# Which PSUM bank a tile gets: the one freed last, or the one that has been free longest

## Chip, cores and metric

The kernel runs on one core of a Trainium2 chip. The metric is the time of one execution on the device in microseconds (us), taken as the median of several runs. The core's engines are named as in the profile: PE (TensorE's matmuls), PEld (TensorE's weight loads), DVE (VectorE), ACT (ScalarE), POOL (GpSimd) and SP (SyncE, which here issues the DMAs).

## What is computed

Three blocks follow each other: an attention with RMS norms on q and k, a gated MLP that mixes over tokens, and a token and channel mixer. Batch 4, 12 heads of 64, 448 tokens, model width 768.

```python
q_n, k_n = (rmsnorm(q, g_q), rmsnorm(k, g_k))
scores = scale * np.matmul(q_n, k_n.transpose(0, 1, 3, 2))
attn = np.exp(scores - np.max(scores, axis=-1, keepdims=True))
x = np.matmul(attn / (np.sum(attn, axis=-1, keepdims=True) + 1e-09), v)
...
h = np.maximum(x @ w_in, 0.0)
u, v = (h[..., :d_ff // 2], h[..., d_ff // 2:])
v_s = np.einsum('ts,bsd->btd', w_spatial, layernorm(v)) + b_spatial[None, :, None]
x = (u * v_s) @ w_out
...
u = x + (np.maximum(x.transpose(0, 2, 1) @ w_tok1, 0.0) @ w_tok2).transpose(0, 2, 1)
out = u + np.maximum(u @ w_ch1, 0.0) @ w_ch2
```

## The kernel before

The kernel is not issued as it is written. Each engine call (`nc.tensor.matmul` and so on) is recorded by `Plan.add` (line 159) as an operation with an estimated cost and its dependencies. At the end `Plan.issue` (line 383) lays all operations out in time with a list scheduler, `Plan.place` (line 267), which gives each operation a planned start, and then emits every operation in the order of those starts. All instructions are emitted at line 424, so the profile shows L424 everywhere, and tiles tell the groups apart. Each engine runs its own instructions in that fixed order; between engines only semaphores hold them.

A matmul or a transpose writes a PSUM tile. PSUM has eight banks, and each tile takes one (`Banks`, line 129; `ALL` is 8). `place` hands the banks out: when an operation is about to write the first of a tile, it picks a bank from `free_banks`, a list of pairs (planned time from which the bank is free, bank number); when the last user of a tile is placed, the bank goes back on the list with the time at which that user is planned to be done. The tile is then allocated under the name `bank0` to `bank7` with one buffer each, so that on the chip the first write of a tile waits until all readers of the tile that had this bank before are done. `OWN` reserves four banks for kind "sc", two for "tp" and two for "mm"; a tile of one kind may take a bank beyond its share only while the others keep theirs. The pick is made in lines 332 to 341:

```python
free_banks.sort()
at = free_banks[len(ks) - 1][0]
if at > t:
    heapq.heappush(due[e], (at, i))
    continue
for k in ks:
    n = max(x for x in free_banks if x[0] <= t)
    free_banks.remove(n)
    bank[k] = n[1]
```

The stages, with the PSUM tiles that the profile names:

- Attention (`Attention.slot`, 24 pairs of heads): `sc` are the scores, read by DVE (maximum, `nm`) and by ACT (exponential, `e`); `tp` are transposes, read mostly by ACT into `et`, `over` or `whole` (the transposed q and k); `av` are the values.
- The gated MLP (`moe`), merged into the attention: `vps`, `ups` (read by ACT into `tg`), `sps` (read by DVE), `xps` (read by ACT into `xo`).
- The token mixer (`Tokens`): `h1ps` (read by ACT and DVE into `h`), `u_ps` (added by DVE into `x`), and `tp`.
- The channel mixer: seven products of a Strassen scheme, in `up` (line 1279) with tiles `h2ps`, which DVE adds into the blocks `c`, and in `down` (line 1325) with tiles `o_ps`, which DVE adds into `o` or `u`. `up` has 7 products times 2 batches times 6 tiles, 84 tiles of 9 matmuls each; `down` has 49 tiles of 18 matmuls. Their operands `op` come from ACT (high part) and DVE (low part), and so do the weights `w`. `word` is DVE's conversion of weights, merged into this and the earlier stages. Tiles in `up` and `down` take banks of the kinds "sc", "tp", "sc", "mm" in turn.

Of the kernel before, what the change touches and what calls it, by code (L numbers as in the profile page):

```python
# [110 lines left out]
class Pool:  # L111
# [5 lines left out]
    def tile(self, shape, dtype, tag, name, bufs=2):  # L117
        ring = self.tags.setdefault(tag, [])
        place = f"{tag}_{len(ring) % bufs}"
        t = Planned(lambda: self.pool.tile(shape, dtype, tag=place, bufs=1, name=name))  # L120
        if len(ring) >= bufs:
            t.after = ring[-bufs].users
        elif self.fence is not None:
            t.after = [self.fence]
        ring.append(t)
        return Part(t, shape, dtype)
# [23 lines left out]
class Plan:  # L150
# [116 lines left out]
    def place(self, before, after, lag, weight, tiles=None):  # L267
# [11 lines left out]
        if tiles is not None:  # L279
            opens, closes, users = tiles  # L280
            users = dict(users)
            free_banks = [(0.0, n) for n in range(Banks.ALL)]
# [6 lines left out]
        while placed < len(ops):  # L289
            t, e = min(  # L290
                (free_at[e] if waiting[e] else max(free_at[e], due[e][0][0]), e)
                for e in engines if waiting[e] or due[e])
            free_at[e] = t
            while due[e] and due[e][0][0] <= t:
                i = heapq.heappop(due[e])[1]
                heapq.heappush(waiting[e], (weight[i], i))
            i = heapq.heappop(waiting[e])[1]
            if e == "tensor" and ops[i].parts != parts:

                near = [x for x in waiting[e] if ops[x[1]].parts == parts and x[0] <= weight[i] + NEAR]  # L300
                if not near and parts and not ops[i].parts:
                    near = [x for x in waiting[e] if ops[x[1]].parts and x[0] <= weight[i] + NEAR]
                if near:
                    x = min(near)
                    waiting[e].remove(x)
                    waiting[e].append((weight[i], i))
                    heapq.heapify(waiting[e])
                    i = x[1]
            other = SHARED.get(e)
            if ops[i].port and port <= t and other in due and free_at[other] <= t:  # L310

                free_at[other] = t
                while due[other] and due[other][0][0] <= t:
                    x = heapq.heappop(due[other])[1]
                    heapq.heappush(waiting[other], (weight[x], x))
                if waiting[other] and waiting[other][0][0] < weight[i] and ops[waiting[other][0][1]].port:
                    heapq.heappush(waiting[e], (weight[i], i))
                    e = other
                    i = heapq.heappop(waiting[e])[1]
            if ops[i].port:  # L320
                if port > t:
                    heapq.heappush(due[e], (port, i))
                    continue
                port = t + ops[i].cost
            if tiles is not None and i in opens:
                ks = opens[i]
                kind = ks[0].psum
                spare = len(free_banks) - sum(max(0, n - held[x]) for x, n in Banks.OWN.items() if x != kind)
                if spare < len(ks):
                    blocked.append(i)  # L330
# [4 lines that stand above are left out]
                    heapq.heappush(due[e], (at, i))  # L335
                    continue
                for k in ks:
                    n = max(x for x in free_banks if x[0] <= t)
                    free_banks.remove(n)
                    bank[k] = n[1]  # L340
                held[kind] += len(ks)
            placed += 1
            start[i] = t
            end = t + ops[i].cost
            if e == "tensor":
                end += SWITCH * (ops[i].parts != parts)
                parts = ops[i].parts
            free_at[e] = end
            for s, hop in zip(after[i], lag[i]):
                ready[s] = max(ready[s], end + hop)  # L350
                left[s] -= 1
                if not left[s]:
                    heapq.heappush(due[ops[s].engine], (ready[s], s))
            if tiles is not None:
                for k in closes.get(i, ()):
                    users[k] -= 1
                    if not users[k]:
                        at = end + ops[i].late + TO["tensor"]
                        free_banks.append((at, bank[k]))
                        held[k.psum] -= 1  # L360
                        for x in blocked:
                            heapq.heappush(due["tensor"], (at, x))
                        blocked = []
# [1128 lines left out]
```

## Time and profile before

| | us |
|---|---|
| median of 3 runs | 887.33 |
| the runs | 885.97 to 889.61 |
| the profiled execution, its own time | 887.2 |
| its span, first to last instruction | 885.0 |
| PE busy in the span | 865.1 (98%) |
| DVE, ACT, POOL busy | 681.0, 537.1, 412.4 |

The profile is of one execution. A matmul's end in it is modelled: matmuls overlap, so that one instruction seems to last longer than the step from its start to the next one's start. Idle time of PE is counted from such an end, and a wait is put down to the instruction whose semaphore ended it. Times in views are counted from the start of the span.

### The profile page before, as it was taken

What the parts mean: (1) busy time and instruction counts of PE and PEld (TensorE: products, weight loads), DVE (VectorE), ACT (ScalarE), POOL (GpSimd) and SP (SyncE); (2) the same over time, 40 slices, a digit from 0 to 9 for tenths busy, and PEclk for the clock granted to TensorE, in tenths of its full rate; (3) what the DMA queues carried; (4) which work ended last, traced back from release to release, by engine and by line L of the source; (5) the groups of instructions that cost most, each with busy time, mean ns of one, the idle gap of its engine ahead of it and who ended that gap; (6) DMA issues with size and microseconds to landing.
All of it is one profiled execution on the core that took longest, in us unless ns stands there. A gap on an engine that the chain in (4) does not pass through costs nothing.

```text
span 885.0 us, 15472 instructions
## 1 busy us (share of the span) xinstructions
PE 865.1 (98%) x5018; PEld 718.2 (81%) x5018; DVE 681.0 (77%) x1333; ACT 537.1 (61%) x1278; POOL 412.4 (47%) x541
## 2 busy tenths in 40 slices
PE   7999999999999999999999999999999999999998
PEld 5444567678777787776889999998989999999998
DVE  5799798987777767866366567889889886998973
ACT  5999988778867867866453356555325654343331
POOL 3555655786666646574234123224324108514560
PEclk8999999999999999999999999999999999999999
DMA  6555665566644575344687678776554745661441
GB/s 153 138 148 172 198 185 149 161 183 211 182 131 127 152 216 169 103 128 127 225 252 236 195 227 268 220 245 202 161 160 138 227 125 170 197 188 54 143 152 63
DMA packets 153263, 152.27 MB, mean 172 GB/s; under 512 B 77152, under 2 KB 136352, under 8 KB 153184
## 3 DMA queue, kind: packets, MB, share of 16 engines
q1 hardware_dynamic: 152224, 151.06, 57.2%
q8 instruction: 40, 0.66, 0.3%
q10 hardware_dynamic: 960, 0.23, 0.1%
q14 instruction: 39, 0.32, 0.1%
HBM read 112.44 MB, written 38.80 MB: 171 GB/s over the span
## 4 chain that ended last, share of the span: by engine, by line
PE 79%; DVE 8%; ACT 4%; issue 3%; DMA 3%; POOL 2%; SPq 1%; DVEq 0%; POOLq 0%; ACTq 0%
PE h2ps L424 15%; PE o_ps L424 15%; PE tp L424 9%; PE av L424 7%; PE sc L424 7%; PE vps L424 7%; PE xps L424 6%; PE ups L424 6%; PE sps L424 4%; PE h1ps L424 2%; PE u_ps L424 2%; DVE word L424 1%; DVE c L424 1%; DVE op L424 1%; DVE w L424 1%
## 5 line engine op out<-in xcount | busy, mean ns | idle before, releaser
L424 PE MATMUL h2ps<-op,w 128*128 128x448 f32 x756 | 155.5, 367 | 2.0 <-DVE c L424 2.0
L424 PE MATMUL o_ps<-w,op 128*128 128x384 f32 x882 | 153.6, 334 | 1.6 <-DVE u L424 1.6
L424 PEld LDWEIGHTS o_ps<-w,op 128*128 128x128 f32 x882 | 152.8, 188 | 2.3 <-ACT op L424 1.5
L424 PEld LDWEIGHTS h2ps<-op,w 128*128 128x128 f32 x756 | 141.3, 188 | 14.7 <-DVE c L424 3.7
L424 ACT ACTIVATE e<-sc,nm 112x448 f32<-112x448 f32 x192 | 122.5, 654 | 22.6 <-DVE nm L424 22.3
L424 DVE TENSOR_REDUCE nm<-sc 112x1 f32<-112x448 f32 x192 | 109.4, 614 | 19.6 <-PE sc L424 19.0
L424 POOL TENSOR_TENSOR src<-src 128x384 f32<-128x384 f32 x48 | 61.1, 1283 | 76.5 <-DMA src<-c_d 55.2
L424 ACT ACTIVATE op<-c 128x768 fp32r<-128x768 f32 x49 | 41.5, 847 | 85.5 <-PE o_ps L424 81.9
L424 PEld LDWEIGHTS tp<-ident,e 112*128 112x128 f32 x672 | 72.3, 140 | 24.3 <-ACT et L424 7.2
L424 POOL TENSOR_SCALAR e<-e,sums 112x448 f32<-112x448 f32 x112 | 73.8, 676 | 36.9 <-DVE sums L424 21.2
L424 PE MATMUL tp<-ident,e 112*128 112x112 f32 x672 | 87.1, 262 | 1.9 <-ACT over L424 1.5
L424 ACT ACTIVATE et<-tp 128x448 f32<-128x448 f32 x144 | 71.2, 527 | 18.2 <-PE tp L424 15.6
L424 DVE TENSOR_SCALAR word<-word 128x256 f32<-128x256 f32 (+5 forms) x132 | 57.9, 448 | 24.5 <-ACT word L424 23.4
L424 POOL TENSOR_TENSOR u<-u,o 128x384 f32<-128x384 f32 x28 | 40.3, 1457 | 69.2 <-ACT o L424 38.9
L424 DVE SCALAR_TENSOR_TENSOR word<-raw,word 128x256 uint32<-128x256 uint32 (+2 forms) x132 | 70.7, 541 | 1.3
L424 PE MATMUL ups<-xp,wu 128*128 128x448 f32 x288 | 67.8, 375 | 0.4 <-ACT et L424 0.4
L424 DVE TENSOR_TENSOR op<-c,op 128x768 fp32r<-128x768 f32 x49 | 58.1, 1185 | 10.3 <-ACT op L424 10.3
L424 PE MATMUL av<-et,v 128*64 128x448 f32 x288 | 61.2, 550 | 0.0
L424 DVE TENSOR_TENSOR c<-c,h2ps 128x448 f32<-128x448 f32 x84 | 50.1, 614 | 12.1 <-PE h2ps L424 11.9
L424 PE MATMUL vps<-wv,xp 128*128 128x512 f32 x216 | 59.3, 408 | 0.0
L424 PE MATMUL xps<-wo,g 128*128 128x384 f32 x288 | 58.2, 345 | 0.0
L424 PEld LDWEIGHTS ups<-xp,wu 128*128 128x128 f32 x288 | 52.2, 188 | 5.5 <-issue 1.0
(141 smaller groups left out, 1650.9 us busy)
## 6 DMA issues: line engine op xcount, KB each, us to landing
src<-c_d SPq DMA_DIRECT2D x132, 192.0 KB, 3.1
wu<-wu_d SPq DMA_DIRECT2D x16, 768.0 KB, 4.6
wo<-wo_d SPq DMA_DIRECT2D x16, 768.0 KB, 5.1
raw<-in_moe_w_ch_dram SPq DMA_DIRECT2D x36, 256.0 KB, 3.3
raw<-in_moe_w_ch_dram SPq DMA_DIRECT2D x24, 384.0 KB, 3.6
raw<-in_q_dram SPq DMA_DIRECT2D x48, 112.0 KB, 2.9
u<-u_d SPq DMA_DIRECT2D x28, 192.0 KB, 3.9
out_dram<-u SPq DMA_DIRECT2D x28, 192.0 KB, 1.9
```

What stands on the lines that cost most here:

```text
L424: getattr(getattr(self.nc, op.engine), fn)(*args, **kwargs)
```

## The change

In `place`, the pick takes the least of the pairs that are free by now, in place of the greatest. So a tile gets the bank with the earliest planned free time, and no longer the one with the latest. Nothing else is edited.

```diff
                 for k in ks:
-                    n = max(x for x in free_banks if x[0] <= t)
+                    n = min(x for x in free_banks if x[0] <= t)
                     free_banks.remove(n)
                     bank[k] = n[1]
```

## Rows read from the trace of the kernel before

**Rows 1.** The page: busy time by engine, and granted clock in 40 slices.
```profile
PE 865.1 (98%) x5018; PEld 718.2 (81%) x5018; DVE 681.0 (77%) x1333; ACT 537.1 (61%) x1278; POOL 412.4 (47%) x541
...
PEclk8999999999999999999999999999999999999999
```

**Rows 2.** Busy time by stretch: columns are named in the first line.
```profile
core 0: us, PE busy (x) PEld busy (x) DVE busy (x) ACT busy (x) POOL busy (x), PEclk, DMA share, GB/s
14.00:102.00 88.00, 82.13 (x483) 41.46 (x484) 75.79 (x166) 83.76 (x236) 47.55 (x75) 0.97 0.58 162
102.00:168.00 66.00, 64.87 (x397) 46.79 (x396) 60.64 (x144) 55.09 (x154) 40.57 (x61) 1.00 0.56 159
168.00:490.00 322.00, 321.86 (x1967) 251.26 (x1966) 225.38 (x548) 218.12 (x576) 185.59 (x283) 1.00 0.60 176
490.00:575.00 85.00, 83.67 (x506) 80.25 (x505) 58.81 (x107) 43.68 (x84) 20.43 (x16) 1.00 0.74 228
575.00:726.00 151.00, 149.03 (x731) 136.56 (x730) 132.55 (x206) 72.92 (x127) 41.44 (x33) 1.00 0.61 185
726.00:776.00 50.00, 48.36 (x278) 47.75 (x277) 39.70 (x45) 22.60 (x39) 31.06 (x22) 1.00 0.53 166
776.00:885.00 109.00, 105.52 (x609) 105.10 (x607) 83.39 (x112) 35.34 (x53) 39.84 (x30) 0.99 0.38 120
```

**Rows 3.** Waits of PE, whole span: total us, times, longest us.
```profile
PE h2ps L424 <- DVE c L424: 2.0, 3, 0.7
...
PE o_ps L424 <- DVE u L424: 1.6, 2, 1.2
...
PE xps L424 <- DVE h L424: 0.9, 1, 0.9
...
PE sps L424 <- ACT tg L424: 0.8, 1, 0.8
...
PE ups L424 <- ACT et L424: 0.4, 1, 0.4
...
PE u_ps L424 <- DVE x L424: 0.2, 1, 0.2
```

**Rows 4.** Waits of PE from 14 to 102 us, same columns.
```profile
PE sc L424 <- ACT whole L424: 2.9, 1, 2.9
...
PE tp L424 <- ACT over L424: 1.5, 2, 1.0
PE sc L424 <- ACT e L424: 0.8, 1, 0.8
PE tp L424 <- ACT et L424: 0.7, 1, 0.7
PE tp L424 <- ACT whole L424: 0.3, 1, 0.3
```

**Rows 5.** Waits of ACT from 14 to 102 us: the longest.
```profile
ACT e L424 <- DVE nm L424: 2.3, 4, 1.6
```

**Rows 6.** The page's group of h2ps matmuls: busy us, mean ns, idle before.
```profile
L424 PE MATMUL h2ps<-op,w 128*128 128x448 f32 x756 | 155.5, 367 | 2.0 <-DVE c L424 2.0
```

**Rows 7.** Order of time, 640 to 650 us: start, us, engine, what, idle before.
```profile
640.87 3.04 DVE L424 TENSOR_SCALAR word<-word 128x384 f32<-128x384 f32 x3
...
643.83 0.61 DVE L424 TENSOR_TENSOR c<-c,h2ps 128x448 f32<-128x448 f32 x1
...
644.50 2.09 PE L424 MATMUL h2ps<-op,w 128*128 128x448 f32 x9 [0.56 <-DVE c L424]
```

**Rows 8.** Waits of DVE from 575 to 726 us: the longest.
```profile
DVE c L424 <- PE h2ps L424: 10.7, 16, 1.2
```

**Rows 9.** Order of time, 755 to 778 us.
```profile
759.59 1.76 DVE L424 TENSOR_TENSOR op<-c,op 128x768 fp32r<-128x768 f32 x1
...
761.27 0.54 DVE L424 TENSOR_TENSOR u<-u,o_ps 128x384 f32<-128x384 f32 x1
...
761.96 12.72 PE L424 MATMUL o_ps<-w,op 128*128 128x384 f32 x72 [1.18 <-DVE u L424]
...
775.14 3.19 PE L424 MATMUL o_ps<-w,op 128*128 128x384 f32 x17 [0.46 <-DVE u L424]
```

**Rows 10.** Busy time by stretch around the only long fall of the clock.
```profile
13.00:21.00 8.00, 6.53 (x20) 2.68 (x20) 6.09 (x11) 5.49 (x13) 1.81 (x2) 0.57 0.75 189
21.00:33.00 12.00, 9.85 (x62) 5.22 (x62) 10.37 (x22) 11.91 (x36) 4.94 (x9) 1.00 0.53 148
```

## The prediction, made before the changed kernel ran

> **What bounds the kernel now.** I read the page first: PE is busy for 865.1 us of the 885.0 us span [rows 1], so 19.9 us is all that it is idle, start and end included, and no change of banks alone can give back more than that and a little overlap. Then the busy time by stretch [rows 2], to see who sets the pace where. From 168 to 490 us PE is busy for 321.86 of 322 us: nothing to win. From 14 to 102 us ACT is busy for 83.76 of 88 us, more than PE (82.13): there ACT sets the pace. From 490 us to the end PE leads, with DVE close behind between 575 and 726 us (132.55 of 151 us against PE's 149.03). Third, the waits of PE [rows 3, 4], where each row is to be sorted by one question: does the matmul read what the named instruction wrote, or does that instruction only read the bank that the matmul is about to fill? `h2ps <- DVE c` is of the second kind: DVE adds an older h2ps tile into c, and the waiting matmul reads op and w. So are `o_ps <- DVE u`, `xps <- DVE h`, `sps <- ACT tg`, `ups <- ACT et`, `u_ps <- DVE x` [rows 3], and `tp <- ACT over`, `sc <- ACT e`, `tp <- ACT et`, `tp <- ACT whole` [rows 4]. `sc <- ACT whole` (2.9 us) is data: scores read the transposed q and k. The bank waits come to 2.0 + 1.6 + 0.9 + 0.8 + 0.4 + 0.2 = 5.9 us in rows 3 and 1.5 + 0.8 + 0.7 + 0.3 = 3.3 us in rows 4, together 9.2 us in 14 waits.
>
> **Does the order really stay?** Every pick, before and after, removes one pair whose time is not later than now, and PE's time in the plan never runs backwards. So at any later pick the number of free pairs, and the pairs still to come free, are the same whichever was taken; `at` and `spare` come out alike, and with them every planned start. Only the bank numbers differ, so what changes on the chip is which old readers a tile's first write waits for. Removed: the wait for the reader that the plan freed last, which may be done only just in time by the plan, and late when its engine runs behind. Added: the wait for the reader freed first, which has had the longest time. No instruction, DMA or queue moves. A wait that is already satisfied I price at nothing: h2ps opens 84 tiles, and its 756 matmuls still cost 155.5 / 756 = 206 ns each [rows 6] with all their waits in. No row shows PE with fewer or more waits, so I allow 0.3 us either way for it, below the rounding of the rest.
>
> **What one wait costs.** The idle time is counted from a modelled end: a matmul seems to last 367 ns, while the step is 206 ns [rows 6]. So a wait loses about 0.16 us more than its idle row says, since the overlap is lost as well. I add that where PE leads.
>
> **The sum, stretch by stretch.**
>
> 14 to 102 us: 3.3 us of bank waits. ACT is the bound, and it is not PE that ACT waits for: its longest wait is on DVE's maximum, 2.3 us [rows 5]. That maximum needs PE's scores, so the gain lies between 0 and 2.3 us; I take 0, because an earlier PE only meets the same ACT queue at the next `et` or `e`.
>
> 102 to 168 us: the sps and ups waits, 0.8 + 0.4, plus 2 x 0.16 = 1.5 us. PE is busy for 64.87 of 66 us, but DVE for 60.64 and ACT for 55.09 [rows 2], so part will come back as waits for these. Between 0 and 1.5 I take 0.8 us.
>
> 490 to 575 us: xps and u_ps, 0.9 + 0.2 + 2 x 0.16 = 1.4 us. DVE has room there (58.81 of 85 us [rows 2]). Bounds 0.7 (half of it lost to the next operand) and 1.4; I take 1.3 us.
>
> 575 to 726 us: three waits of h2ps, 2.0 + 3 x 0.16 = 2.5 us. The pattern is in [rows 7]: DVE spends 3.04 us on words, is late with one c, and PE stands for 0.56 us although the operands of the next tile lie ready. What is late next is op, from the same DVE. But outside such bursts DVE waits for PE, 10.7 us in 16 waits [rows 8], so it catches up while PE fills other banks. Bounds 1.3 and 2.5; I take 2.4 us.
>
> 726 to 776 us: two waits of o_ps, 1.18 and 0.46 us [rows 9]. In the first the operand itself was ready only at 759.59 + 1.76 = 761.35 us, and PE began at 761.96: a free bank gives 0.6 of it. The second is 0.46 + 0.16 = 0.6 us. Together 1.2 us, with bounds 0.5 and 2.0 (both idle times, 1.64, and two overlaps of 0.16).
>
> 0.8 + 1.3 + 2.4 + 1.2 = 5.7 us. The profiled execution took 887.2 us, 2.2 us outside its span, and is 0.1 us from the median of the runs (887.33): 887.2 - 5.7 = 881.5 us. The low ends add to 0 + 0.7 + 1.3 + 0.5 = 2.5 us (884.7), the high ends to 2.3 + 1.5 + 1.4 + 2.5 + 2.0 = 9.7 us (877.5).
>
> **The rivals.** About 0.5%, or 4.4 us, is what a measurement of this kernel can tell from no change; so below 882.8 is faster.
>
> *Given back.* The banks come free, but PE soon meets the operands of the same late DVE or ACT. For it speaks DVE's 132.55 of 151 us and 60.64 of 66 us [rows 2]; against it that DVE waits for PE in between [rows 8]. By the low ends of the sum: 884.7 us, inside 0.5%.
>
> *Little changes at all.* Where scores, transposes and the long accumulations of the MLP hold most banks, one or two are free, and oldest and newest are the same. That may be so up to 490 us, but not in up and down, where one tile is filled and one or two are read. It would leave 1 us or less: 887 us.
>
> *More than I sum.* The opening gains too, as if the waits for ACT had held DVE's maximum up: the high ends, 877.5 us.
>
> *Slower: the oldest bank belongs to a late DVE.* The list is sorted by planned times. If ACT keeps to the plan and DVE is late, the newest bank may really be free (an ACT reader) and the oldest not (a DVE reader). Its place is 102 to 490 us, where the banks are full and PE has no idle time that could hide anything; its price is a wait like those seen, 0.7 us each at most for h2ps [rows 3]. It decides from the point at which DVE is later than the oldest bank has been free: DVE can be 3.04 us late [rows 7]. In up a tile takes 9 x 206 ns = 1.9 us, so a bank that comes round after six others has been free for some 11 us, and the wait cannot arise; in the attention the age is shorter. To end over 4.4 us above 887.2 it would take (4.4 + 5.7) / 0.7, about 14 such waits, as many as all bank waits now. Then 892 us.
>
> *Slower: the clock.* The granted clock fell once for long: over 13 to 21 us it averaged 0.57 [rows 10], where PE had stood for the 2.9 us of its data wait [rows 4]. Such a fall costs (1 - 0.57) x 8 = 3.4 us of full clock. With banks taken round robin, PE would have to stand between tile groups often enough for the clock to fall in a stretch where PE leads; three falls against the gain give 887.2 - 5.7 + 10.3 = 891.8 us. Against it: from 21 to 33 us PE was busy for only 9.85 of 12 us, in short pieces, and the clock stayed at 1.00 [rows 10], as in every later full slice [rows 1]. The Trainium skill has a rule that speaks for this rival and against the change: "TensorE: Matmul & The Clock Gate", section "A second HAM failure mode: psum-queue depth-cycling", tells of a kernel whose cycling through PSUM banks left TensorE idle so often between groups that its clock went up and down. By that rule the time would be that of this rival; the trace disagrees so far, since the idle pieces between groups are here already with the old choice, the clock holds, and the change can only shorten them.
>
> **How the numbers follow.** Forecast (gain of 4.4 to 7 us): 0.50. More: 0.08. Given back (1 to 4.4 us): 0.30. Little changes: 0.05. Slower by a late DVE: 0.05. Slower by the clock: 0.02. So faster 0.58, within 0.5% 0.35, slower 0.07. The range reaches from the high ends to the case in which hardly anything changes: 877.8 to 887.5 us; beyond it lie the two slower cases and a little on either side.
>
> **What would show it.** In the profile after: no `h2ps <- DVE c` and no `xps <- DVE h` among PE's waits; PE busy for over 150 of 151 us in the up stretch, which ends earlier; the opening as long as before, with PE idle there now for data; the order of instructions on each engine unchanged; the clock at 1.00 after 21 us. Wrong would be: the bank waits gone and the same idle time under op or w (given back); new waits of PE on DVE readers between 102 and 490 us (late DVE); a gain that appears before 102 us (I took ACT for the bound there); or a change in the steps of single matmuls, which nothing here foresees.

## The result, and the profile after

The changed kernel takes 877.79 us (median of 4 runs, 877.64 to 878.35) against 887.62 us for the kernel before beside it: a ratio of 0.9889 with a 95% interval of 0.9868 to 0.9910, so 9.8 us less, give or take 1.9. The forecast was 881.5 us, and its range began at 877.8. The direction was right and the size was not: 9.8 us where 5.7 were forecast.

The profiled execution took 878.35 us with a span of 876.2 us, 8.8 us shorter than the span before. The order of instructions on every engine is the same. First the page after, for [rows 1].

```profile
PE 862.7 (98%) x5018; PEld 720.7 (82%) x5018; DVE 678.3 (77%) x1333; ACT 536.7 (61%) x1278; POOL 414.5 (47%) x541
...
PEclk8999999999999999999999999999999999999999
```

PE does the same 5018 matmuls in 2.4 us less busy time: part of what a wait costs stands in busy time, since ends are modelled. Busy time by stretch from 168 us on, in the columns of [rows 2]:

```profile
168.00:490.00 322.00, 322.00 (x1970) 252.24 (x1969) 227.53 (x549) 218.01 (x576) 186.33 (x281) 1.00 0.59 176
490.00:575.00 85.00, 84.53 (x512) 82.05 (x512) 60.84 (x109) 44.81 (x86) 20.38 (x16) 1.00 0.76 241
575.00:726.00 151.00, 151.00 (x752) 140.45 (x751) 134.07 (x214) 75.33 (x132) 41.81 (x34) 1.00 0.61 180
726.00:776.00 50.00, 50.00 (x291) 50.00 (x290) 40.55 (x47) 20.33 (x33) 33.98 (x25) 1.00 0.69 209
```

Where [rows 2] had 149.03 of 151 us and 48.36 of 50 us, PE now fills both stretches. The waits of PE, whole span, for [rows 3, 4]:

```profile
PE sc L424 <- ACT whole L424: 3.3, 2, 2.8
...
PE av L424 <- ACT et L424: 1.3, 3, 0.5
PE tp L424 <- ACT over L424: 0.6, 1, 0.6
PE tp L424 <- POOL wide L424: 0.6, 1, 0.6
...
PE sc L424 <- ACT e L424: 0.5, 1, 0.5
PE tp L424 <- DVE x L424: 0.5, 1, 0.5
...
PE sc L424 <- ACT over L424: 0.3, 1, 0.3
```

All six rows of [rows 3] are gone: h2ps, o_ps, xps, sps, ups and u_ps wait for no reader any more. What is left after the start are waits for data (`whole`, `et`, `wide`, `x`) and 1.4 us of bank waits (`tp <- over`, `sc <- e`, `sc <- over`), the last of them at 146 us. One more row of before is gone that [rows 4] passes over, in the same view from 14 to 102 us:

```profile
PE tp L424 <- issue: 1.7, 2, 1.0
```

The profile names no releaser for these two waits. They are bank waits too: the row stands, with 1.7 or 1.8 us, in every run here that takes the newest bank in the opening, or one free for 0.3 us, and in none of the others. The second of them ends at 95.60 us, 0.10 us after ACT has copied a `tp` tile into `et`.

The burst of [rows 7] is still there, in the order of time:

```profile
633.68 9.48 PE L424 MATMUL h2ps<-op,w 128*128 128x448 f32 x46
...
636.45 3.04 DVE L424 TENSOR_SCALAR word<-word 128x384 f32<-128x384 f32 x3
...
639.40 0.61 DVE L424 TENSOR_TENSOR c<-c,h2ps 128x448 f32<-128x448 f32 x1
```

DVE is as late as before, 3.04 us of words ahead of c, and PE runs through it without a gap, at the same step as before (9.48 / 46 = 206 ns). That is the whole mechanism in three lines.

Since the order is the same, the same matmul can be looked up in both traces. Its start, in us from the start of the span, and by how much PE is ahead:

| matmul | before | after | ahead |
|---|---|---|---|
| av, the last one of the opening | 96.48 | 95.54 | 0.9 |
| ups after the wait for et | 163.67 | 162.45 | 1.2 |
| sps that read late behind et | 388.09 | 386.29 | 1.8 |
| xps after the wait for h | 493.40 | 490.52 | 2.9 |
| tp before up | 568.39 | 564.71 | 3.7 |
| h2ps, the last one that waited | 673.15 | 666.72 | 6.4 |
| o_ps, first wait | 761.96 | 753.96 | 8.0 |
| o_ps, second wait | 775.14 | 766.44 | 8.7 |

### The profile page after: what moved, and what is told of

It is laid out like the page before. It is cut to its first block, busy times and chain, and to the rows that moved or that the text cites. A ratio compares the mean times of both kernels' runs of the same rounds, so it can differ in the third digit from the quotient of the medians.

```text
span 876.2 us, 15461 instructions
## 1 busy us (share of the span) xinstructions
PE 862.7 (98%) x5018; PEld 720.7 (82%) x5018; DVE 678.3 (77%) x1333; ACT 536.7 (61%) x1278; POOL 414.5 (47%) x541
## 4 chain that ended last, share of the span: by engine, by line
PE 82%; DVE 2%; ACT 1%; issue 1%; POOL 0%; DMA 0%; DVEq 0%; POOLq 0%
PE o_ps L424 17%; PE h2ps L424 17%; PE tp L424 7%; PE xps L424 7%; PE ups L424 6%; PE av L424 6%; PE vps L424 5%; PE sc L424 5%; PE sps L424 4%; PE h1ps L424 3%; PE u_ps L424 3%; DVE wpart L424 0%; DVE word L424 0%; DMA raw<-in_moe_w_out_dram 0%; DVE nm L424 0%
```

## The experiments

All of them keep the plan and the order of the kernel before; only the banks differ, and in three of them DVE gets extra work. Theory A: the gain is the sum of waits for late readers that are gone, each in its own place, and what counts is only how long the bank has been free by the plan. In the diffs `k.mixer` marks the tiles h2ps and o_ps. Theory A was tested first by parts.

**The mixer alone, and all but the mixer.**

```diff
-                    n = max(x for x in free_banks if x[0] <= t)
+                    pick = min if k.mixer else max
+                    n = pick(x for x in free_banks if x[0] <= t)
```

> The oldest bank for the tiles of the channel mixer alone (h2ps and o_ps), the newest for all others. Theory A (the gain is the waits for late readers that are gone, each in its own place): PE keeps its pace of the kernel before until the up stage and then gains what the changed kernel gained there and in down, 0.6 + 0.8 + 1.0 + 0.3 + 1.6 + 0.7 = 5.0 us, so about 882.5 us. Rival B (a use of all eight banks by turns helps by itself, wherever tiles are opened): gain in proportion to the tiles opened by the new rule; 133 of some 600 tiles, about 2 us, 885.5 us. Rival C (what is won early is only handed on): the whole gain appears here or none of it, 878 or 887 us.

Measured: 881.91 us against 888.78, ratio 0.9922 (0.9910 to 0.9934), 6.9 us less. In the trace PE starts like the kernel before up to 575 us and is 5.1 us ahead at the end, by steps of 0.9, 0.8, 1.0, 0.3 (h2ps) and 1.6, 0.7 (o_ps), after a lag of 0.2 us. PE's waits still hold the bank waits of the earlier stages, and none of h2ps or o_ps:

```profile
PE tp L426 <- ACT over L426: 1.5, 2, 1.0
PE xps L426 <- DVE h L426: 0.9, 1, 0.9
PE sc L426 <- ACT e L426: 0.8, 1, 0.8
PE tp L426 <- ACT et L426: 0.7, 1, 0.7
PE sps L426 <- ACT tg L426: 0.7, 1, 0.7
```

The complement swaps `min` and `max`.

> The complement: the oldest bank for every tile but h2ps and o_ps, the newest for those two. Theory A: the gain of the changed kernel up to the channel mixer, 8.8 - 5.0 = 3.8 us, stays to the end, about 883.7 us, and the waits h2ps <- DVE c and o_ps <- DVE u are back among PE's waits. Rival B: about 7 of 9 us, 880.5 us. Rival C: the mixer's own waits swallow the early gain (DVE and ACT are then no earlier), 887 us.

Measured: 884.20 us against 888.78, 0.9945 (0.9932 to 0.9959), 4.6 us less. Now the mixer's waits are the ones that are back:

```profile
PE h2ps L426 <- DVE c L426: 2.1, 3, 0.8
...
PE o_ps L426 <- DVE u L426: 1.2, 1, 1.2
```

Theory A stands, and rivals B and C fall: each part gains in its own place and keeps it, 6.9 + 4.6 = 11.5 us, beside 10.8 us for the kernel with an age of 3 us on the same chip and 9.4 us for the changed kernel on another (below). The parts are a little more than the whole, by no more than the intervals allow.

**How old must a bank be?** The newest bank among those that are free by the plan for at least an age, and the oldest where there is none:

```diff
-                    n = max(x for x in free_banks if x[0] <= t)
+                    aged = [x for x in free_banks if x[0] <= t - 1000]
+                    n = max(aged) if aged else min(x for x in free_banks if x[0] <= t)
```

> The newest bank among those that by the plan have been free for at least 1 us; the oldest where there is none. Theory A (what counts is by how much a reader may be late against the plan before PE feels it): the waits of readers that are less than 1 us late go, those behind bursts of 2 to 3 us on DVE stay in part; 4 to 6 us of the 9, 881 to 884 us. Rival B (turns through all banks): few banks are used by turns, little gain, 886 us.

> As the run before with an age of 3 us, the length of the longest burst of DVE read ahead of the change. Theory A: nearly all of the gain, 878 to 879 us, though banks that have been free for longer lie unused. Rival B: still little, 884 to 886 us.

> The newest bank among those that by the plan have been free for 0.3 us. Theory A (a wait ends as many us earlier as its bank is older, and the waits that the change removed cost 0.3 to 1.6 us each): between the kernel before and the kernel with 1 us, 3 to 6 us less than before, with waits h2ps <- DVE c still there but shorter. If the plan's own lateness is small beside one tile's length: nearly as good as 1 us, 879 to 880 us, since passing over the newest bank already means one tile more.

Measured: with 0.3 us 882.88 against 887.40, 4.5 us less (0.9957, 0.9942 to 0.9971); with 1 us 879.25 against 888.78, 9.5 us less (0.9889, 0.9874 to 0.9903); with 3 us 877.94 against 888.78, 10.8 us less (0.9877, 0.9864 to 0.9890). So it is age that pays, and 1 us buys most of it, where I had expected 4 to 6 us. At 0.3 us PE still waits in `up`,

```profile
PE h2ps L425 <- DVE c L425: 2.1, 3, 0.8
```

as in [rows 3], and for as long, where I had expected shorter waits; the rows of o_ps, xps, sps, ups and u_ps are gone. From 1 us on the h2ps row is gone too. In the profile of the run with 1 us PE lost 1.1 us to a load of wo; that is a transfer and not a bank.

**Is it the number of banks, or which bank it is?** In the changed kernel, h2ps and o_ps go through banks 0 to 2, and take another only where none of these is free (4 of 133 tiles):

```diff
+                    now = [x for x in free_banks if x[0] <= t]
+                    n = min([x for x in now if x[1] < 3] or now) if k.mixer else min(now)
```

> As the changed kernel, but the tiles of the channel mixer (h2ps, o_ps) go by turns through banks 0 to 2 alone. Theory A (only the age of a bank counts): in up a bank comes round after two other tiles, 2 x 1.85 us less the 1 us or so that DVE reads, so some 2.5 us old; nearly as much as the 3.0 us of DVE's burst. The mixer keeps 4 of its 5 us: 878 to 880 us. Rival B (it takes all eight banks): the mixer's 5 us are lost, 883 to 884 us.

Measured: 877.80 us against 887.97, 0.9897 (0.9878 to 0.9916). Three banks by turns do as well as eight in the mixer: rival B falls again. The bank numbers that the planner of each kernel gives to the tiles of up, in the order in which they are opened, say the same. In the kernel before, two banks alternate over long stretches (404040, 707070); with 0.3 us mostly two; with 1 us mostly three (261261); with 3 us mostly four; in the changed kernel eight. The waits for c are there with two and gone from three on. So in up an older bank and one more bank in turn are the same thing, and no run here separates them.

The control renames the banks of the kernel before:

```diff
-            t.bank = n
+            t.bank = (3 * n + 2) % 8
```

> A control: the kernel before with its eight banks renamed (bank n becomes bank 3n + 2 modulo 8), so every tile waits for the same readers in another bank. Theory A (it is who had the bank that counts): the time of the kernel before within 0.2%. Rival F (some banks are dearer than others, or neighbours disturb each other): another time, by a good part of the 10 us.

Measured: 888.11 us against 887.40, 1.0008 (0.9999 to 1.0017). No difference can be told; rival F falls. And the changed kernel beside it:

> The changed kernel once more, beside the kernel before on this chip, for comparison with the runs by parts and by age: 877.5 to 878.5 us, 9.5 to 10.8 us less than before.

Measured: 877.98 us against 887.40, 0.9891 (0.9876 to 0.9906).

**The opening alone.**

```diff
+                    pick = min if t < 95000 else max
+                    n = pick(x for x in free_banks if x[0] <= t)
```

> The oldest bank only for tiles that the plan opens before 95 us, the newest later. As the prediction had it (ACT sets the pace of the opening): no gain at 102 us and none in the end, the time of the kernel before. Theory A without that exception: PE is 0.9 to 1.2 us ahead at 102 us, as in the two kernels with the oldest bank there, and keeps it: 0.9 to 1.2 us less than before.

Measured: 886.87 us against 887.97, 0.9987 (0.9979 to 0.9996), 1.1 us less, with an interval from 0.4 to 1.9. So the opening does give about 1 us, where the prediction took nothing. The length of the first fall of the clock, which differs between executions (last section), does not make the difference: among the runs with a mean granted clock of 0.998 the mean times are 886.5 us (6 runs) against 887.4 (8 runs). Why it is little all the same is seen in PE's order of time, 24 to 33 us. Before:

```profile
26.60 1.01 PE L424 MATMUL sc<-whole 64*112 64x448 f32 x4 [0.83 <-ACT e L424]
27.54 0.60 PE L424 MATMUL tp<-ident,wide 112*128 112x112 f32 x4
...
29.51 0.89 PE L424 MATMUL tp<-ident,e 112*128 112x112 f32 x7 [0.98 <-ACT over L424]
...
31.71 1.73 PE L424 MATMUL av<-et,v 128*64 128x448 f32 x8
```

and after:

```profile
25.46 1.01 PE L424 MATMUL sc<-whole 64*112 64x448 f32 x4
27.10 0.60 PE L424 MATMUL tp<-ident,wide 112*128 112x112 f32 x4 [0.63 <-POOL wide L424]
...
29.28 1.44 PE L424 MATMUL sc<-whole 64*112 64x448 f32 x4 [0.53 <-ACT e L424]
...
31.54 1.72 PE L424 MATMUL av<-et,v 128*64 128x448 f32 x8 [0.39 <-ACT et L424]
```

The two bank waits are gone, PE is 1.1 us ahead at `sc`, and then it stands for its data (`wide`, `et`) and once for a bank that ACT still reads (`e`); at `av` 0.2 us is left. This is the rival "given back", and here it is real. Only small rests are kept: up to 95 us they come to 0.5 us, and the last wait without a releaser (95.60 us) brings the rest of the 0.9 us at 96 us.

**A late reader made on purpose.** Six times in up, DVE gets extra work just ahead of an addition that reads an h2ps tile (once in each product but the first, whose tiles ACT reads):

```diff
+            if op.engine == "vector" and op in held_up:
+                for _ in range(10):
+                    self.nc.vector.tensor_tensor(self.spare, self.spare, self.spare, op=ALU.mult)
```

> The kernel before (newest bank) with six pieces of extra work on DVE in the up stage, ten 128 x 128 products each, about 2 us, each just ahead of one addition that reads an h2ps tile; the plan does not know of them. Theory A: PE runs into each late reader, because the bank it holds is the next to be used; with up to 1 us of slack each costs 1 to 2 us, 6 to 12 us in all, and the rows h2ps <- DVE c grow from 2.0 us by as much. Rival D (DVE has 18 us of room in 151, so it does not matter which bank is taken): 0 to 2 us more than before.

> The changed kernel (oldest bank) with the same six pieces of work on DVE. Theory A: a bank has been free for some 11 us, the delay is taken up by banks in waiting, and PE does not see it: the time of the changed kernel within 1 us, no row h2ps <- DVE c. Rival D: the same 0 to 2 us more as in the kernel with the newest bank. Rival E (with DVE at 145 of 151 us the operands come late): as much more as the kernel with the newest bank, 6 us or over, with PE idle under op and not under c.

The pieces came out longer than meant: 3.2 to 4.2 us each, in place of 2. Newest bank: 908.27 us against 887.97, 20.3 us more, and h2ps <- DVE c at 16.0 us; some 5 us of it are the clock (last section). Oldest bank: 890.03 us against 887.97, so 12.1 us more than the same kernel without the pieces (877.98 on another chip). The first piece, newest bank:

```profile
608.62 3.93 DVE L426 TENSOR_TENSOR ident<-ident 128x128 f32<-128x128 f32 x10
612.47 0.61 DVE L431 TENSOR_TENSOR c<-c,h2ps 128x448 f32<-128x448 f32 x1
613.14 7.09 PE L431 MATMUL h2ps<-op,w 128*128 128x448 f32 x26 [2.30 <-DVE c L431]
```

and with the oldest:

```profile
599.65 12.53 PE L431 MATMUL h2ps<-op,w 128*128 128x448 f32 x61
...
603.48 4.21 DVE L426 TENSOR_TENSOR ident<-ident 128x128 f32<-128x128 f32 x10
...
607.61 0.61 DVE L431 TENSOR_TENSOR c<-c,h2ps 128x448 f32<-128x448 f32 x1
```

With the newest bank PE stands until the late addition is done; with the oldest it works through 4.21 us of delay. In the traces the first three pieces cost the kernel with the oldest bank nothing (PE stays 7.4 us ahead of the kernel before up to 673 us), while they cost the other one 9 us by then. The later ones do cost, under other names, so the time that theory A expected (within 1 us) failed, while no row h2ps <- DVE c came up:

```profile
PE o_ps L431 <- ACT op L431: 5.6, 1, 5.6
...
PE h2ps L431 <- DVE op L431: 1.7, 2, 1.0
```

That is rival E, in part: banks in waiting hide a late reader, and not a late operand. The last run leaves out the sixth piece, which stands right at the end of up:

> The changed kernel with five of the six pieces of DVE work (3.2 us each by the trace), without the last, which stood at the end of the up stage. Theory A: inside the stage a late reader costs nothing as long as DVE catches up; PE meets DVE only in the operands, 2 us in all by the trace of the run with six: 879 to 881 us. The 6 us that the sixth piece cost came from the operands of down, which read the last blocks c, and not from banks. If instead every piece costs alike, 888 us.

Measured: 885.70 us against 887.40, that is 7.7 us more than without the pieces (877.98 us beside it): the expectation of 1 to 3 us failed. By the starts of the same matmuls in the traces of the two kernels, PE loses 3.4 us inside up, where 2 were foreseen, and then 3.5 us at the passage to down:

```profile
728.82 0.96 DVE L431 TENSOR_TENSOR op<-c,op 128x768 fp32r<-128x768 f32 x1 [0.84 <-ACT op L431]
...
728.84 0.62 PE L431 MATMUL o_ps<-w,op 128*128 128x384 f32 x2 [2.66 <-ACT op L431]
```

DVE had not caught up: it was busy for 140.62 of 151 us in up, 6.6 us more than in the changed kernel, and down's operands are made of the c that it still owed. I had put the 5.6 us on the sixth piece alone. Behind this wait the clock falls, which costs another 1.7 us (last section); the profiled execution, at 886.64 us, is 0.9 us above the median. A backlog is put off by the banks, and paid where the next stage reads its result.

## Why the prediction missed, step by step

By the traces, PE's gain in each stretch of [rows 2] (how far the first matmul behind the bound is ahead, less the same at the bound before; from the start of the span for the first row) beside the forecast, in us:

| stretch | forecast | its bounds | measured |
|---|---|---|---|
| 14 to 102 | 0 | 0 to 2.3 | 0.94 |
| 102 to 168 | 0.8 | 0 to 1.5 | 0.37 |
| 168 to 490 | no term | none | 0.48 |
| 490 to 575 | 1.3 | 0.7 to 1.4 | 1.71 |
| 575 to 726 | 2.4 | 1.3 to 2.5 | 3.15 |
| 726 to 776 | 1.2 | 0.5 to 2.0 | 2.13 |

- *The order stays*: right, and so was pricing satisfied waits at nothing. In the traces even more of PE's weight loads carry a semaphore wait than before (1,026 against 828), the step of h2ps is 206 ns in both, and the time falls all the same: how long a wait's bank has been free matters, not how many waits there are.
- *Which waits are bank waits* [rows 3, 4]: right for the rows that were sorted. All six groups of [rows 3] are gone, and the mixer and the rest each gained by their own. The sum left out the two waits `tp <- issue`, 1.7 us in the opening.
- *726 to 776 us.* The step that failed is the operand: I read the DVE op that ends at 761.35 us [rows 9] as that of the waiting tile. In the trace after, that same op starts at 753.01 us and ends at 754.78, and the tile starts at 753.96: it was the next tile's operand. Nothing but the bank held PE, so the whole 1.18 us and the lost overlap came back, where 0.6 was counted.
- *What one wait costs.* This term was mis-sized where PE leads: a wait cost not 0.16 but about 0.26 us more than its idle row. The first matmul behind it starts 0.16 us further ahead than the row says, and the next one follows 0.3 us later in place of 0.21 (603.55 and 603.86 us in the kernel before), which is lost too. In up the three waits and a fourth, which left no idle row (0.3 us at 673.15 us), make nearly all of the 3.15 us; all three stretches from 490 us on lie above their high ends. The discounts for what would be given back were not needed there.
- *14 to 102 us.* ACT as the bound was the right reading, and most of each wait did come back; zero was too low. The sign that I had named as wrong, a gain before 102 us, did appear. *102 to 168 us*: given back as in the opening.
- *168 to 490 us.* "PE busy for 321.86 of 322 us: nothing to win" put this stretch at nothing. Of the 0.48 us, 0.4 came at the sps that starts at 388.09 us: its wait for ACT's `et` had left no idle time on PE, because the modelled end of the matmul before covered it. It stands in the trace of before on PEld (0.35 us).
- Of the rivals, *more than I sum* met the number, 877.5 us by the high ends, but by luck and not by its mechanism: the opening gave 0.94 of its 2.3 us, and ACT's wait for DVE's maximum did not shrink (2.3 us in [rows 5], 2.7 after). The rest came from the waits that cost more and from the stretch without a term. The chance of 0.08 was too small, because I discounted each term where PE leads for the same fear. The range ended 0.3 us above that rival, with no room for the runs' own spread, and the result lies 0.01 us outside it.
- *A late DVE* and *the clock*: neither appeared in the changed kernel. With extra DVE work both showed with the newest bank; with the oldest, the clock fell once, behind a wait for an operand.

In all, the traces give 0.94 + 0.37 + 0.48 + 1.71 + 3.15 + 2.13 = 8.78 us, 8.84 us with the last 0.06 in the tail, where 5.7 were forecast. The further microsecond of the medians (9.8) lies in which executions were profiled: that of the kernel before (887.2 us) is 0.4 us below the median beside the changed kernel, and that of the changed kernel (878.35 us) is the slowest of its four runs, 0.6 us above their median. Why executions of the kernel before spread more, 885.5 to 890.1 us over all its runs in this study against 877.3 to 878.4 us over eight of the changed one, was not tested. That the newest bank hands each small delay on to PE would make such a spread.

## What to carry to other kernels

Where a planner hands out buffers that wait for their last reader, give the one that has been free longest: here it cost nothing that a trace shows, and it covered readers that were late against the plan, by up to 4.21 us of extra work, while they were late by less than the buffer's age. A few buffers by turns were enough (three here, where two were not), and an age of 1 us bought most of the gain. It hides late readers alone; a stage in which the same engine also makes the operands pays the rest of the delay later.

When a gain is summed from waits, ask for each wait whose operand it is by its place in the order, look for waits that the profile gives no releaser or no idle time on PE, and do not discount every term for the same reason: then the sum errs to one side.

## What the runs showed of the clock

The granted clock fell in the kernel with extra DVE work and the newest bank, in the middle of the dense up stage:

```profile
575.00:612.00 37.00, 35.20 (x172) 31.80 (x171) 32.93 (x47) 18.90 (x33) 11.72 (x9) 1.00 0.72 226
612.00:618.00 6.00, 4.86 (x16) 4.38 (x17) 5.53 (x10) 2.62 (x5) 1.14 (x1) 0.72 0.43 133
```

It was granted in full up to the wait of 2.30 us shown above and averaged 0.72 over the 6 us around and behind it, so for part of them it was at the lower of its two levels, 1.2 GHz. Such a fall costs (1 - 0.72) x 6 = 1.7 us of full clock. It came twice more in that kernel, some 5 us in all. With the oldest bank and the six pieces the clock fell once, around the wait of 5.6 us (0.83 from 720 to 740 us), and with five pieces once, behind the wait of 2.66 us; inside up it stayed at 1.00 in both. In the kernel before, the waits of up to 1.2 us that the change removed did not bring it down. So the rival of the clock was the wrong way round: where a reader was late, it was the newest bank with which the clock fell inside up. The Trainium skill, in "TensorE: Matmul & The Clock Gate", section "A second HAM failure mode: psum-queue depth-cycling", tells of a kernel that cycles through PSUM banks, in which TensorE's short idle times between groups make the clock go up and down; here the kernel that cycles through all eight banks kept 1.00 from 168 to 776 us.

The fall at the start [rows 10] is not always equally long: over 13 to 21 us the clock averaged 0.57 in the kernel before and in the changed one, and 0.79 in others, among them the opening alone and the control. In these two PE was 1.0 and 1.3 us ahead of the kernel before at 21 us. The control has the waits of the kernel before, so this is not the banks' doing, and single profiles of the opening are not to be compared to a microsecond without a look at this row.
